# Three shifted terms in place of four for VectorE's exponentials, in a fused attention and MLP kernel

## The chip, the cores and the metric

The program runs on one core of a Trainium2 chip. The metric is the device time of one execution in microseconds (us), as a median over runs. The kernel before takes 758.89 us, the median of 3 runs (758.78 to 759.5).

## The reference

One transformer block in its parallel form: layer norm, then attention and an MLP side by side, summed with the input. The sizes are S = 2048 tokens, D = 512, H = 32 heads of 16 columns, F = 1792.

```python
xn = layernorm(x)
q, k, v = split(xn @ wqkv)                      # 32 heads of 16
p = softmax(q @ k.T * 16**-0.5)                 # 32 x 2048 x 2048 scores
attn = (p @ v) @ wo
y = layernorm(xn)
mlp = gelu(y @ w1 + b1) @ w2 + b2
return x + attn + mlp
```

So 134 million exponentials have to be taken, and that is what the kernel is built around.

## The kernel before

**Units and tiles.** Heads are taken four at a time. A *group* g is four heads against 512 queries (there are 32 groups), and a *tile* (g, k) is one group against 128 keys: four score blocks of 128x512, one for each head, which the text calls *units*. There are 32 x 16 x 4 = 2048 units. TensorE computes a unit's scores into one PSUM bank (`qk`, L1162), four row strips at a time. The softmax isn't normalised in advance: V has a column of ones beside its 16 (18 columns a head in `va`), so the sum of the exponentials comes out of the same product, and the result is divided by it later (`build_opost`, L1524).

**Two engines take the exponential.** ScalarE takes two or three units in one instruction (`build_tile`, L1382, output `p_sb`), in alternating pairs of banks, and each unit's weights are then multiplied with V (`build_pv`, L1180). VectorE takes whole tiles in another way (`build_dve`, L1467, and `dve_terms`, L1488). It adds a level to the scaled score and stores it as int16 (L1479, one *conversion* for each unit). Read as fp16, those bits are a stepwise linear 2**x. Three more copies, shifted by constants (L1500, one *shift* of 128x2048 for each term), have their kinks elsewhere, and the sum of the four is a smoother exponential. The sum is never formed: all four go into the product with V, one PV row (four matmuls) for each term, two rows to a piece of work.

```python
TERMS = 4                                                       # L34
SHIFT = (0, 190, 422, 740)                                      # L35
rows = [(va[:, k, :], bits(ib[sl]))]                            # L1492
    rows.append((va[:, k, :], bits(tb[x])))                     # L1507
    if len(rows) == 2 or t == TERMS - 1:                        # L1508
        o = add("PE", pen(len(rows)), lambda rows=rows: pv(g, k, rows), ...)
```

The scores of a VectorE tile *ride*: with each of ScalarE's score tiles, TensorE computes one unit for VectorE into another bank (`ride`, L1259). `KD` (L517) lists the key blocks that VectorE may take in a group. ScalarE takes the others first, and then what is left in `KD`.

**What sets the order.** The kernel is written as operations with an engine, a duration, dependencies and resources. A planner (`_Plan.run`, L134) lists them by a greedy rule when the program is built, and a table of numbers (`PICK`, L645) overrides its choice at some steps. The chip then runs each engine's list in order, and semaphores hold the dependencies. The planner also places matmuls on zeros where TensorE would otherwise be idle (`fill`, L1825; the 128x128 ones of the start stand on L1852, the later ones on L1857), and a zero strip beside some score tiles (`zeros`, L1310).

**Buffers.** The shifted copies lie in a ring of `NTB` = 4 tiles (`tb`, L564); a shift waits until the PV row that read its slot last is done. Other rings: q of a pair of groups in `NQB` = 4 slots (L568), W1 columns in `NW1` = 5, attention outputs in `NON` = 8 (L525). GpSimd adds x and b2 into `acc` by DMA (`sums`, L1717) and checks the softmax sums (L1570 to L1573).

**The end.** The last group is divided on VectorE in two halves (`build_opost_last`, L1580: transpose, reciprocal, multiply, transpose). `build_final` (L1773) adds the last products with Wo to `acc` for four blocks of 128 tokens: for three of them an fp32 identity matmul puts `acc` into the bank (L1784) and ScalarE copies it out (L1805), for one VectorE adds it (L1802). A flag is summed (L1622), every engine reads it and branches past a general version of the kernel.

## Time and profile before

| what | value |
|---|---|
| median of 3 runs | 758.89 us |
| the profiled execution's own time | 758.38 us |
| its span in the trace | 756.6 us |
| TensorE busy | 724.6 us (96%) |
| VectorE busy | 708.1 us (94%) |
| ScalarE busy | 735.4 us (97%) |
| GpSimd busy | 54.8 us (7%) |

Busy time is the time in which at least one instruction of the engine ran. The span goes from the first instruction to the last, barriers at the end included; 1.8 us of the execution's time lie around it. Three engines are close to full, so a share alone doesn't tell which of them sets the time: that is read from who waits for whom, stage by stage.

### The profile page before, as it was taken

The page shows a single profiled execution, that of the slowest core. Times are in us where ns is not written, and L with a number is a line of the kernel's source. Part 1 is how long each engine was busy: PE and PEld are TensorE (multiplying, and loading weights), DVE is VectorE, ACT ScalarE, POOL GpSimd, SP SyncE. Part 2 cuts the span into 40 slices and gives each one's busy share as a digit, 9 for nine tenths or more (in the row PEclk, how much of TensorE's full clock was granted, in tenths as well). Part 3 has the DMA queues.
Part 4 walks back from the last instruction along what each step waited for, and adds up shares of the span by engine and source line. Part 5 has one row for each costly group of instructions (what it writes and reads, how often), then busy time and mean ns, then how long its engine had stood idle before and what let it go on. Part 6 is the DMA issues. An engine that isn't in the chain of part 4 may idle for free.

```text
span 756.6 us, 23209 instructions
## 1 busy us (share of the span) xinstructions
PE 724.6 (96%) x9898; PEld 244.0 (32%) x9900; DVE 708.1 (94%) x1217; ACT 735.4 (97%) x663; POOL 54.8 (7%) x93
## 2 busy tenths in 40 slices
PE   8999999999999999999999999999999899999997
PEld 3443333343332323333333333332233222333332
DVE  8999999999999997999999989889999999879995
ACT  6999999999999999999999999999999999999995
POOL 4400000000121000000110000000002000100010
PEclk9999999999999999999999999999999999999999
DMA  7334321111255111121243121222114001332001
GB/s 223 86 72 130 73 68 28 35 48 50 51 122 109 52 31 40 52 49 30 68 103 75 37 70 29 54 62 71 33 46 109 14 22 35 86 79 52 17 7 45
DMA packets 79067, 46.54 MB, mean 62 GB/s; under 512 B 53428, under 2 KB 70772, under 8 KB 78960
## 3 DMA queue, kind: packets, MB, share of 16 engines
q1 hardware_dynamic: 73392, 36.11, 18.1%
q0 software_dynamic: 4608, 8.39, 4.9%
q8 instruction: 78, 1.28, 0.7%
q10 hardware_dynamic: 960, 0.52, 0.2%
q14 instruction: 29, 0.24, 0.1%
HBM read 30.01 MB, written 7.19 MB: 49 GB/s over the span
## 4 chain that ended last, share of the span: by engine, by line
ACT 38%; PE 34%; DVE 15%; issue 12%; DMA 1%; POOL 0%; DVEq 0%; ACTq 0%; POOLq 0%
ACT p_sb L1382 33%; PE ps L1162 11%; PE ps L1180 11%; PE ps L604 9%; DVE it L1500 5%; DVE x_sb L1479 5%; ACT ht L1681 2%; DVE it L1479 1%; ACT ht L1700 1%; DVE ht L1669 1%; PE ps L1857 0%; DVE osb L1535 0%; PE ps L609 0%; DVE va L1062 0%; DMA ldram<-osb 0%
## 5 line engine op out<-in xcount | busy, mean ns | idle before, releaser
L1382 ACT ACTIVATE p_sb<-ps 128x1536 bf16<-128x1536 f32 (+1 forms) x619 | 695.3, 1271 | 6.3 <-PE ps L1162 4.4
L1162 PE MATMUL ps<-qz,kt 32*128 32x512 bf16 x2048 | 310.2, 382 | 21.8 <-ACT p_sb L1382 12.7
L1479 DVE TENSOR_SCALAR x_sb<-ps 128x512 int16<-128x512 f32 x420 | 277.8, 682 | 13.6 <-PE ps L1162 12.1
L1500 DVE TENSOR_SCALAR it<-x_sb 128x2048 int16<-128x2048 int16 x315 | 211.2, 685 | 2.9 <-PE ps L1180 1.8
L1162 PEld LDWEIGHTS <-kt 32*128 32x128 bf16 x2048 | 85.3, 91 | 275.8 <-issue 265.8
L1180 PE MATMUL ps<-p_sb,va 128*32 128x512 bf16 x1520 | 150.4, 388 | 1.0 <-DVE va L1062 0.4
L1180 PE MATMUL ps<-it,va 128*32 128x512 f16 x1692 | 137.8, 381 | 1.1 <-DVE va L1062 0.6
L1180 PEld LDWEIGHTS <-va 128*32 128x32 bf16 x3632 | 76.0, 94 | 132.1 <-issue 106.7
L1317 PE MATMUL ps<-ones_bf,zeros_bf 32*128 32x512 bf16 x297 | 106.5, 382 | 0.0
L1479 DVE TENSOR_SCALAR it<-ps 128x512 int16<-128x512 f32 x108 | 72.3, 682 | 5.3 <-PE ps L1162 5.2
L604 PE MATMUL ps<-w_sb,ht 128*32 128x512 bf16 x896 | 59.7, 381 | 0.0
L604 PE MATMUL ps<-yT,w_r 128*32 128x512 bf16 x896 | 58.1, 381 | 0.0
L1500 DVE TENSOR_SCALAR it<-it 128x2048 int16<-128x2048 int16 x81 | 54.5, 682 | 1.2 <-PE ps L1180 0.7
L1180 PE MATMUL ps<-x_sb,va 128*32 128x512 f16 x420 | 41.4, 384 | 0.1
L1721 POOL DMA_DIRECT2D wkv<-in_A_x_dram x16 | 11.9, 741 | 297.7 <-DVE ot L1735 266.6
L1669 DVE TENSOR_SCALAR ht<-ps,b_sb 128x512 bf16<-128x512 f32 x40 | 29.8, 744 | 2.2 <-PE ps L604 2.1
L1317 PEld LDWEIGHTS <-zeros_bf 32*128 32x128 bf16 x297 | 25.9, 91 | 10.5 <-issue 9.3
L604 PEld LDWEIGHTS <-w_r 128*32 128x32 bf16 x896 | 21.0, 96 | 24.7 <-issue 10.0
L604 PEld LDWEIGHTS <-ht 128*32 128x32 bf16 x896 | 20.5, 96 | 23.2 <-issue 9.5
L1570 POOL TENSOR_SCALAR okt<-lc 128x128 f32<-128x128 f32 (+1 forms) x4 | 2.7, 666 | 314.3 <-DMA lc<-ldram 314.3
L1857 PE MATMUL ps<-ones_bf,zeros_bf 128*32 128x512 bf16 x252 | 22.8, 384 | 0.0
L1535 DVE COPY osb<-ps 128x512 f32<-128x512 f32 x31 | 21.2, 683 | 0.7 <-PE ps L1180 0.5
(98 smaller groups left out, 330.3 us busy)
## 6 DMA issues: line engine op xcount, KB each, us to landing
rlb<-rdram SPq DMA_DIRECT2D x31, 256.0 KB
w_r<-in_B_w_dram SPq DMA_DIRECT2D x56, 128.0 KB
wkv<-in_A_x_dram POOLq DMA_DIRECT2D x16, 256.0 KB, 3.5
wkv<-in_B_b_dram POOLq DMA_DIRECT2D x16, 256.0 KB, 4.1
qz<-zdram SPq DMA_DIRECT2D x30, 128.0 KB
ydram<-ys SPq DMA_DIRECT2D x16, 128.0 KB
zdram<-qc SPq DMA_DIRECT2D x15, 128.0 KB
w_sb<-in_B_w_dram SPq DMA_DIRECT2D x1, 1792.0 KB
```

Source lines behind the costliest of these rows:

```text
L604: I(nc.tensor.matmul(dst[32 * j:32 * j + 32], lhsT=lhsT[:, 32 * j:32 * j + 32], rhs=rhs, start=start, stop=stop, tile_position=(0, 32 * j)))
L1162: I(nc.tensor.matmul(ps[:, bank, :], lhsT=kt[lo:lo + 32, s // 2, k * P:(k + 1) * P], rhs=qz[lo:lo + 32, (qt * NB + s // 2) % NQB, s % 2, : ...
L1180: I(nc.tensor.matmul(ps[32 * j:32 * j + 32, o_bank[g], :], lhsT=vals[:, h * VS:h * VS + 32], rhs=wts(j), start=pv_done[g] == 1, stop=end, ...
L1317: I(nc.tensor.matmul(ps[:, o_bank[g], :], lhsT=zeros_bf[32 * j:32 * j + 32, :], rhs=ones_bf[32 * j:32 * j + 32, :], start=False, stop=Fals ...
L1382: exp_inst.append(I(nc.scalar.activation(p_sb[:, s0:s1, :].rearrange("p a b -> p (a b)"), ps[:, b0:b0 + n, :].rearrange("p a b -> p (a b)" ...
L1479: I(nc.vector.tensor_scalar(out=ib[sl][:, j, :], in0=ps[:, pool.bank(key), :], scalar1=LEVEL, scalar2=0.0, op0=ALU.add, op1=ALU.max))
L1500: I(nc.vector.tensor_scalar(out=tb[x].rearrange("p j q -> p (j q)"), in0=ib[sl].rearrange("p j q -> p (j q)"), scalar1=float(SHIFT[t]), sc ...
L1535: e0 = add("DVE", dve(QW), lambda: I(nc.vector.tensor_copy(osb[:, i2, :], ps[:, o_bank[g], :])), pvs + before, pr - 1000, rel=(o_done(g),))
L1669: I(nc.vector.tensor_scalar(out=hq[:, fc, :], in0=ps[:, misc.bank(key), :], scalar1=b1_sb[:, fc:fc + 1], scalar2=None, op0=ALU.add))
L1681: I(nc.scalar.activation(out=hv, in_=hv, func=AF.Gelu_apprx_tanh, scale=1.0))
L1721: xb_ = add("POOL", 1.0, lambda: I(nc.gpsimd.dma_start(out=acc[:, c, :], in_=x2[qi * P:(qi + 1) * P, :])), wait, pr - 30, lat=XL, nb=pr - 45)
L1857: I(nc.tensor.matmul(ps[32 * j:32 * j + 32, bank, :], lhsT=zeros_bf[:, 0:32], rhs=ones_bf[:], start=new, stop=new, tile_position=(0, 32 * ...
```

## The change

**Terms.** VectorE's exponential has three terms, with shifts 0, 342 and 683, and each shifted term is multiplied with its own weighted copy of V. The weights 1, 203/256 and 161/256 are applied to V when V leaves PSUM: for the key blocks in `KD`, VectorE writes two more copies into the new tile `vw`. GpSimd writes the weight into `vw`'s columns of ones, so that the sums are weighted too.

**Sizes.** `KD` goes from seven key blocks to five, so that `vw` has room; the rings shrink from 4 to 2 (`NTB`), 8 to 7 (`NON`), 5 to 4 (`NW1`) and 4 to 3 (`NQB`).

**End and start.** The last group is transposed at once and divided in two halves. Two blocks of tokens, not one, are added on VectorE, so that two identity matmuls are left. GpSimd executes a drain after its last DMA. The zeros of the start wait for an operation of another engine, and some are left out.

**Order.** The planner's constants and `PICK` are new.

```diff
-TERMS = 4
-SHIFT = (0, 190, 422, 740)
-LEVEL = 1024.0 * (15.0 - 2.41262)
+TERMS = 3
+SHIFT = (0, 342, 683)
+WEIGHT = (1.0, 203.0 / 256.0, 161.0 / 256.0)
+LEVEL = 1024.0 * (15.0 - 1.6403)
-    KD = (2, 4, 6, 8, 10, 12, 14)
+    KD = (6, 8, 10, 12, 14)
-    NPU, NI, NTB, NON, NW1 = 15, 5, 4, 8, 5
+    NPU, NI, NTB, NON, NW1 = 15, 5, 2, 7, 4
+    vw = const.tile([P, TERMS - 1, len(KD), VROW], BF, name="vw")
-    NQB = 4
+    NQB = 3
-    D1 = ((1, 7), (1, 8), (1, 13), (1, 14))
+    D1 = ((1, 6), (1, 8), (1, 12), (1, 14))
     PICK = {
-        29: 30, 69: 45, 83: 62, 93: 95, 101: 54, 104: 57, 107: 55, 117: 348, 118: 79, 128: 69, 130: 72,
+        30: 33, 43: 143, 65: 44, 93: 95, 99: 57, 108: 80, 131: 81, 136: 190, 138: 72, 139: 69, 141: 378,
...
+    def c_vw():
+        for t in range(1, TERMS):
+            I(nc.gpsimd.memset(vw[:, t - 1, :, 0:H * VS].rearrange("p k (h r) -> p k h r", r=VS)
+                               [:, :, :, DH:VS], WEIGHT[t]))
...
+    mk_vw = add("POOL", 1.6, c_vw, (r1_op[4],), 0.0)
...
+            def fvw(t, b=b, ks=ks, key=key, pool=pool):
+                x = KD.index(ks[0])
+                I(nc.vector.tensor_scalar(
+                    out=vw[:, t - 1, x:x + len(ks), 8 * b * VS:8 * (b + 1) * VS].rearrange(
+                        "p t (h r) -> p t h r", r=VS)[:, :, :, 0:DH],
+                    in0=ps[:, pool.bank(key), :].rearrange("p (t h r) -> p t h r", t=TQ, r=DH)
+                    [:, ks[0] % TQ:ks[-1] % TQ + 1:2],
+                    scalar1=WEIGHT[t], scalar2=None, op0=ALU.mult))
...
-        rows = [(va[:, k, :], bits(ib[sl]))]
+        rows = [(va_t(g, k, 0), bits(ib[sl]))]
-            rows.append((va[:, k, :], bits(tb[x])))
+            rows.append((va_t(g, k, t), bits(tb[x])))
+            deps.append(vw_of(g, k, t))
...
+        def f0():
+            I(nc.vector.transpose(out=ta[:], in_=ps[:, o_bank[g], :]))
+            I(nc.vector.reciprocal(out=rl_t[:], in_=tav[:, :, DH]))
...
+        def last():
+            I(nc.gpsimd.dma_start(out=acc[:, c, :], in_=b2_all, accum_op=ALU.add))
+            if qi == NT - 1:
+                I(nc.gpsimd.drain())
...
+        BARE = (1, 2)
-            dep = [acc_op[c], mk_idf] + h_use[(NQT - 1) % 2] + ([exp_prev[0]] if c else [])
-            if c != 2:
+            dep = [acc_op[c], mk_idf] + h_use[(NQT - 1) % 2] + ([qk_prev[0]] if c else [])
+            if c not in BARE:
-                if c == 2:
+                if c in BARE:
...
+            gate = max([x for x in I.trail if x[0] < t - 0.3 and x[1] in ("DVE", "ACT", "POOL")],
+                       key=lambda x: x[0], default=None) if t0 <= T0 and t > GATE else None
+            skip = COLD < t < WARM and len(got) % 2
```

Counted over the lists of instructions that the two programs have: conversions go from 528 to 556 (132 tiles to 139), shifts from 396 to 278, ScalarE's exponentials of 1536 columns from 282 to 276 and those of 1024 from 337 to 332 (1520 units to 1492). PV rows of VectorE's tiles go from 528 to 417, of ScalarE's from 380 to 373. Later zero matmuls (L1857 before) go from 252 to 332, zero strips from 297 to 323. Writes of `vw` on VectorE: 24, of which 8 have 128 columns and 16 have 256; on GpSimd there are 6 memsets.

VectorE after the first token block's output is added (`ot<-ps,wkv`, some 300 us into the program): conversions stand as `128x512`, shifts as `128x2048`, `osb` is the copy of a finished group. Before:

```order
L1735 TENSOR_TENSOR ot<-ps,wkv 128x512
L1479 TENSOR_SCALAR x_sb<-ps 128x512
L1535 COPY osb<-ps 128x512
L1479 TENSOR_SCALAR x_sb<-ps 128x512
L1500 TENSOR_SCALAR it<-x_sb 128x2048 x2
L1479 TENSOR_SCALAR x_sb<-ps 128x512
L1500 TENSOR_SCALAR it<-it 128x2048
L1479 TENSOR_SCALAR x_sb<-ps 128x512 x2
L1500 TENSOR_SCALAR it<-x_sb 128x2048
L1479 TENSOR_SCALAR x_sb<-ps 128x512 x2
L1500 TENSOR_SCALAR it<-x_sb 128x2048
```

And with the change:

```order
L1773 TENSOR_TENSOR ot<-ps,wkv 128x512
L1570 COPY osb<-ps 128x512
L1534 TENSOR_SCALAR it<-x_sb 128x2048 x2
L1513 TENSOR_SCALAR x_sb<-ps 128x512 x2
L1534 TENSOR_SCALAR it<-it 128x2048 x2
L1513 TENSOR_SCALAR x_sb<-ps 128x512 x2
L1534 TENSOR_SCALAR it<-x_sb 128x2048
L1513 TENSOR_SCALAR x_sb<-ps 128x512 x2
```

A tile now has two shifts to its four conversions, and the two slots of the ring are written in turn, so two to four conversions stand between two writes of a slot.

VectorE at the end of the program, from the last output copy before the final group. Before:

```order
L1735 TENSOR_TENSOR wkv<-ps,wkv 128x512
L1590 STREAM_TRANSPOSE ht<-ps 128x256
L1595 RECIPROCAL rl_t<-ht 128x8
L1596 TENSOR_TENSOR ht<-ht,rl_t 128x256
L1599 STREAM_TRANSPOSE ons<-ht 128x256
L1590 STREAM_TRANSPOSE ht<-ps 128x256
L1595 RECIPROCAL rl_t<-ht 128x8
L1596 TENSOR_TENSOR ht<-ht,rl_t 128x256
L1599 STREAM_TRANSPOSE ons<-ht 128x256
L1802 TENSOR_TENSOR yT<-ps,wkv 128x512
L1622 TENSOR_REDUCE flag_i<-ps 1x1
```

And with the change:

```order
L1584 TENSOR_TENSOR ont<-osb,rlb 128x512
L1534 TENSOR_SCALAR it<-it 128x2048 x2
L1622 STREAM_TRANSPOSE ht<-ps 128x512
L1623 RECIPROCAL rl_t<-ht 128x16
L1630 TENSOR_TENSOR ht<-ht,rl_t 128x256
L1633 STREAM_TRANSPOSE ons<-ht 128x256
L1630 TENSOR_TENSOR ht<-ht,rl_t 128x256
L1633 STREAM_TRANSPOSE ons<-ht 128x256
L1841 TENSOR_TENSOR yT<-ps,wkv 128x512 x2
L1656 TENSOR_REDUCE flag_i<-ps 1x1
```

The second half's transpose and reciprocal are gone from between the two multiplies, one more output block stands behind them, and the last tile's two shifts stand right ahead of the final transpose.

VectorE where the second quarter of V leaves PSUM (`va`), with the change; before, the row of `va` is followed by other work and `vw` isn't there:

```order
L849 TENSOR_SCALAR yT<-x_sb,mv,r_85 128x512 x3
L1074 CAST va<-ps 128x4x8x16
L1085 TENSOR_SCALAR vw<-ps 128x8x16 x2
L876 CAST xnT<-ps 128x4x128
```

The two copies for key block 6 are written before anything else of VectorE's, and the bank is given back only after them.

## Rows read from the trace of the kernel before

**Rows 1.** The page's first part: busy time, share of the span, instructions.

```profile
span 756.6 us, 23209 instructions
...
PE 724.6 (96%) x9898; PEld 244.0 (32%) x9900; DVE 708.1 (94%) x1217; ACT 735.4 (97%) x663; POOL 54.8 (7%) x93
```

**Rows 2.** Busy us by stretch: PE, PEld, DVE, ACT, POOL; clock, DMA share, GB/s.

```profile
13.00:60.00 47.00, 44.23 (x793) 18.11 (x792) 44.90 (x95) 45.40 (x50) 11.95 (x27) 1.00 0.31 83
60.00:105.00 45.00, 42.36 (x677) 15.01 (x681) 43.87 (x77) 43.69 (x41) 0.00 (x0) 1.00 0.35 92
...
150.00:200.00 50.00, 48.84 (x790) 17.25 (x787) 48.24 (x80) 49.84 (x45) 0.00 (x0) 1.00 0.19 50
...
sum 733.00, PE 708.69 PEld 236.15 DVE 694.22 ACT 726.68 POOL 48.23; mean PE 47.25 PEld 15.74 DVE 46.28 ACT 48.45 POOL 3.22
```

**Rows 3.** ScalarE's groups by shape: busy us, mean ns, idle before them.

```profile
L1382 ACT ACTIVATE p_sb<-ps 128x1536 bf16<-128x1536 f32 x282 | 424.2, 1504 | 2.3 <-PE ps L1162 1.9
L1382 ACT ACTIVATE p_sb<-ps 128x1024 bf16<-128x1024 f32 x337 | 356.9, 1077 | 4.1 <-PE ps L1162 2.5 <-ACT p_sb L1382 0.2
```

**Rows 4.** ScalarE's timeline, merged by line: start, length, instructions; both shapes in one.

```profile
99.56 161.54 ACT L1382 ACTIVATE p_sb<-ps 128x1536 bf16<-128x1536 f32 x142
```

**Rows 5.** VectorE's groups by shape.

```profile
L1479 DVE TENSOR_SCALAR x_sb<-ps 128x512 int16<-128x512 f32 x420 | 277.8, 682 | 13.6 <-PE ps L1162 12.1
L1500 DVE TENSOR_SCALAR it<-x_sb 128x2048 int16<-128x2048 int16 x315 | 211.2, 685 | 2.9 <-PE ps L1180 1.8
L1479 DVE TENSOR_SCALAR it<-ps 128x512 int16<-128x512 f32 x108 | 72.3, 682 | 5.3 <-PE ps L1162 5.2
L1500 DVE TENSOR_SCALAR it<-it 128x2048 int16<-128x2048 int16 x81 | 54.5, 682 | 1.2 <-PE ps L1180 0.7
...
L981 DVE TENSOR_SCALAR qz<-ps,mask 128x128 bf16<-128x128 f32 x1 | 0.3, 343 | 0.0
```

**Rows 6.** TensorE's timeline: a PV piece of one row, and one of two.

```profile
717.71 0.40 PE L1180 MATMUL ps<-p_sb,va 128*32 128x512 bf16 x4
...
718.90 0.60 PE L1180 MATMUL ps<-it,va 128*32 128x512 f16 x8
```

**Rows 7.** TensorE's groups by shape: the zero matmuls after the start.

```profile
L1857 PE MATMUL ps<-ones_bf,zeros_bf 128*32 128x512 bf16 x252 | 22.8, 384 | 0.0
```

**Rows 8.** Timeline of the end, all engines.

```profile
743.63 2.37 ACT L1382 ACTIVATE p_sb<-ps 128x1024 bf16<-128x1024 f32 x2
...
746.39 2.84 PE L1784 MATMUL ps<-wkv,ident_f 128*128 128x512 f32 x6
746.57 0.45 DVE L1590 STREAM_TRANSPOSE ht<-ps 128x256 f32<-128x256 f32 x1
...
749.28 0.45 DVE L1599 STREAM_TRANSPOSE ons<-ht 128x256 bf16<-128x256 bf16 x1
...
750.68 0.39 PE L604 MATMUL ps<-wo_l,ons 128*32 128x512 bf16 x4
...
751.19 0.69 DVE L1802 TENSOR_TENSOR yT<-ps,wkv 128x512 bf16<-128x512 f32 x1 [1.46 <-PE ps L604]
```

**Rows 9.** The closing line of the program: duration min/median/max, first and last start.

```profile
L1909 POOLq DRAIN  x3: 40/107/2683, 753.1 to 756.3; - x3
L1909 SPq DRAIN  x3: 7/7/13, 754.8 to 756.0; - x3
```

**Rows 10.** Stretches behind the last matmul; columns as in rows 2.

```profile
753.00:754.00 1.00, 0.00 (x0) 0.00 (x0) 0.00 (x0) 0.00 (x0) 0.00 (x0) 0.73 0.22 70
754.00:755.00 1.00, 0.00 (x0) 0.00 (x0) 0.00 (x0) 0.00 (x0) 0.00 (x0) 0.50 0.11 25
```

**Rows 11.** Timeline of the start: VectorE and GpSimd.

```profile
6.43 0.16 DVE L825 TENSOR_SCALAR wv<-mv 128x2 f32<-128x2 f32 x1
...
6.67 0.79 POOL L829 TENSOR_TENSOR r<-wv,mhalf 128x2 f32<-128x2 f32 x1 [0.60 <-DVE wv L825]
...
7.50 0.74 DVE L846 TENSOR_SCALAR yT<-x_sb,mv,r 128x512 bf16<-128x512 bf16 x2 [0.59 <-POOL r L829]
```

More of the change, by code (lines that the diff above doesn't have):

```diff
@@ L200, in run @@
             op.end, op.at = end, t
+            self.trail.append((end, op.eng, self.last.get(op.eng)))
             free[op.eng] = end
@@ L1065, in fve, with va_t, vw_of @@
                     in_=ps[:, pool.bank(key), :].rearrange("p (t h r) -> p t h r", t=TQ, r=DH)))
+            ks = [k for k in KD if k // TQ == tq]
+            free = (pool.giver(key),) + ((one,) if b else ())
             va_op[b, tq] = add("DVE", dve(QW), fve, (m, mk_va, mk_ok), pr - 500,
-                               rel=(pool.giver(key),) + ((one,) if b else ()))
+                               rel=() if ks else free)
+            def fvw(t, b=b, ks=ks, key=key, pool=pool):
[6 more added lines that the diff above has]
+                    scalar1=WEIGHT[t], scalar2=None, op0=ALU.mult))
+            o = va_op[b, tq]
+            for t in range(1, TERMS if ks else 1):
+                o = vw_op[b, tq, t] = add(
+                    "DVE", dve(len(ks) * P), lambda t=t, f=fvw: f(t), (o, mk_vw), pr - 500,
+                    rel=free if t == TERMS - 1 else ())
     def va_of(g, k):
         return va_op[g % NS // 2, k // TQ]
+    def va_t(g, k, t):
+        return va[:, k, :] if t == 0 else vw[:, t - 1, KD.index(k), :]
+    def vw_of(g, k, t):
+        return vw_op[g % NS // 2, k // TQ, t]
     blocks = [(g, kg) for kg in range(FO) for g in range(2)] + [
@@ L1723, in sums @@
             nb=pr - 45)
-        return add("POOL", 1.0, lambda: I(nc.gpsimd.dma_start(
-            out=acc[:, c, :], in_=b2_all, accum_op=ALU.add)), (xb_,), pr - 20, lat=XL)
+        def last():
+            I(nc.gpsimd.dma_start(out=acc[:, c, :], in_=b2_all, accum_op=ALU.add))
+            if qi == NT - 1:
+                I(nc.gpsimd.drain())
+        return add("POOL", 1.0, last, (xb_,), pr - 20, lat=XL)
     def heads(qt, bs, cs):
@@ L1848, in fill, with fn @@
                         continue
[L1850 removed]
+            gate = max([x for x in I.trail if x[0] < t - 0.3 and x[1] in ("DVE", "ACT", "POOL")],
+                       key=lambda x: x[0], default=None) if t0 <= T0 and t > GATE else None
+            skip = COLD < t < WARM and len(got) % 2
+            def fn(opened=o_open[-1] if o_open else None, spot=spot, gate=gate, skip=skip):
                 if t0 <= T0:
[L1852 to L1853 removed]
+                    if skip:
+                        return None
+                    m = I(nc.tensor.matmul(ps[:, OB, :], lhsT=zeros_bf[:], rhs=ones_bf[:],
+                                           start=True, stop=True))
+                    if gate:
+                        tc.add_manual_dep(m.ins, gate[2].ins.name, SYNC_DEP, reason="its turn")
+                    return m
                 bank = spot[0] if spot else o_bank[opened]
```

60 lines of the change are left out of this document (30 added, 30 removed), and 57 rows, old and new, of the table PICK.

## The prediction

> **What bounds the kernel now.** I read the page's busy times first, to see which engines are candidates [rows 1]: ScalarE with 97% of the span, TensorE with 96%, VectorE with 94%. That leaves it open, so the busy times by stretch come next [rows 2]. From 150 to 200 us ScalarE works 49.84 of 50 us, TensorE 48.84, VectorE 48.24. Over the 733 us from 13 to 746 it works 726.68; TensorE 708.69, some of it on zeros; VectorE 694.22. ScalarE's idle time of 6.3 us is the least, and it falls mostly early: 1.6 of 47 us up to 60 us, 1.3 of 45 us up to 105 us, where VectorE is at 96% and 97%. The groups of ScalarE say what ended it [rows 3]: 6.4 us ahead of all 619 exponentials, mostly a wait for the scores (L1162). So ScalarE's exponentials set the time, TensorE and VectorE sit just under it, and a change pays by what it takes off ScalarE, provided that the other two still feed it. What is left of the span is a start of some 11 us and an end of some 10 us behind the last exponential, two chains of their own.
>
> **ScalarE.** By the counts of the two programs it gives 28 units away: 6 exponentials of three units, 5 of two. The price of a unit comes from a long stretch without a gap [rows 4]: 142 exponentials, 71 of each shape, so 355 units, in 161.54 us, 0.455 us a unit. (The 1504 and 1077 ns of [rows 3] overlap their neighbours and are no price.) 28 x 0.455 = **12.7 us less** on the engine that sets the time.
>
> **VectorE.** It takes 7 tiles more and still works less. 118 shifts go, at 0.685 us each: 80.8 us less. 28 conversions come, at 0.682: 19.1 us more [rows 5]. The 24 writes of `vw` have no row; their ends are 0.343 us, the nearest scaled copy out of PSUM of 128 columns, and 0.682, the conversion of 512 [rows 5]. I take 0.343 for the 8 narrow ones and 0.45 for the 16 of 256 columns, nearer to the narrow end: 9.9 us (8.2 to 16.4). The sum is 51.8 us less, 708.1 to some 656. The `vw` writes of the first head pair, some 2.5 us, fall into the full stretch before 105 us; the first four VectorE tiles, which lie there too, have one shift less each, 2.7 us. I set the two against each other and count nothing.
>
> **TensorE.** PV rows of VectorE's tiles go from 528 to 417, of ScalarE's from 380 to 373: 118 rows less. A piece of two rows lasts 0.60 us and one of a single row 0.40 [rows 6], so a row is worth about 0.2 us: 24 us less. The zeros grow from 252 to 332 matmuls, 22.8 us by their group [rows 7], so 7 us more by the mean; the zero strips lie beside scores. TensorE ends some 17 us lower. Neither engine is the bound, so this counts for nothing by itself; what it can do is to feed ScalarE in better time. Of the 6.3 us of idle, 2.9 lie before 105 us, where VectorE was full. I take half of that back, **1.5 us**; the ends are a gain of all 6.3 and, since the new order was not seen on the chip, a loss of as much.
>
> **The end.** The last exponential ends at 746.0 [rows 8]. Three identity matmuls then hold TensorE for 2.84 us, up to 749.2; VectorE has the second half divided at 749.73; the last product starts at 750.68, the added block leaves VectorE at 751.88. With the change there are two identity matmuls (1.9 us, to 748.3 or, with four products ahead, 748.5), and on VectorE one transpose of 512 columns takes the place of two of 256 at 0.45 [rows 8]. At 0.7 to 0.9 us for that one, 0.25 for the reciprocal and 0.88 for a half, the halves stand at some 748.5 and 749.35. The products behind them end near 750.0 rather than 751.07, and VectorE's second addition near 750.8 rather than 751.88, although it has two to do: **1.05 us less** (0.4 to 1.5).
>
> **The drain.** The program closes with a drain on GpSimd that starts at 753.1 and lasts 2683 ns, to 755.8, while SyncE, which has the most to wait for, is at its own drain at 754.8 [rows 9]. So GpSimd holds the closing barrier back by 0.95 us. The other two drains of GpSimd last 107 and 40 ns, and no DMA of GpSimd stands behind the new drain. I take it that the long one is then done in the last block, where GpSimd is idle nearly throughout, and that the closing one is short: **0.95 us less** (0 to 0.95). Behind the new drain stand the checks of the sums and the flag; 2.7 us there are hidden, since GpSimd's work is 55 us in all [rows 1].
>
> On what a drain costs the Trainium skill speaks against this change: "VectorE: DVE Perf Modes", section "The DRAIN you can't avoid", calls the drains at a program's start and end a constant of about 12 ns on all five engines. By that page the early drain would bring nothing, and the sum would stand 0.95 us higher. The row disagrees for GpSimd, 2683 ns, and agrees for SyncE, 7 to 13 ns.
>
> **The start.** The second normalisation pair waited for a small addition at 6.43, which stood behind a wide operation, and for GpSimd's 0.79 us from 6.67; its tiles were written from 7.50 [rows 11]. The addition now stands first, so the pair can come some 0.45 us earlier, and the first scores need it. **0.4 us less**; the ends are 0.6 less and, with zeros that now wait and are partly left out, 1.0 more. The 6 memsets of `vw` on GpSimd stand ahead of the third group's rsqrt and cost at most 2 us there; they come where GpSimd works 12 of 47 us [rows 2], so nothing. A ring slot fewer for q and W1 leaves a pair of groups (733/16, some 45 us) for loads: nothing.
>
> **The sum.** 758.38 (the profiled execution, 0.5 under the median of the runs) - 12.7 - 1.5 - 1.05 - 0.95 - 0.4 = 741.8, say **742.0 us**. By the ends of the unknown terms the likeliest case reaches from 737.0 to 747.0 (not all ends fall together).
>
> **Rivals.**
> *The other engines' slack reaches ScalarE in full.* All 6.3 us of its idle go, which is 4.8 beyond the forecast: 737. If the price of a unit fell too, since small delays of the scores may hide in it, each 1% (0.455 to 0.450) would be 7 us on the 1492 units that are left; half a per cent gives 733.5. For it: 52 us less on VectorE, 17 on TensorE. Against it: from 150 to 200 us, with VectorE at 96%, ScalarE has no idle to give [rows 2], and pieces of TensorE's other work still stand between scores.
>
> *The smaller ring gives part back.* A shift must now wait for the PV row that read the slot two shifts before. Before, with four slots, 396 shifts waited 4.1 us in all [rows 5]. If the wait becomes 0.3 us for each of 278, it is 83 us, about VectorE's whole slack (742 - 656 = 86): conversions come late, their banks too, and TensorE's scores with them. Half of ScalarE's 12.7 us given back leaves 748, all of it 755.
>
> *Slower: the same stall, past its point.* The ring is the place, VectorE's list the mechanism: 86 us of slack over 139 tiles are 0.62 us a tile, and each 0.1 us beyond it costs 14 us. From 0.75 us a tile on the gain is gone; at 0.9 the time is 742 + 0.28 x 139 = 781. For it: the two last rows of a tile are read by TensorE, which runs in order, 1 to 2 us after the shift. Against it: two to four conversions, 1.4 to 2.7 us, stand between two writes of a slot.
>
> *Slower: TensorE's clock.* The granted clock is 1.00 in every stretch up to 753, and 0.50 from 754 on [rows 2, 10], the lower of the two levels (1.2 of 2.4 GHz), after the last matmul at 751. TensorE now has 17 us less to do. If the clock fell in the middle, its work, some 690 of 718 us, would take twice as long, so each us of the course at the lower level costs about 0.95: 17 us of it eat the gain, and 24 give 765. Against it: the 80 more zeros stand in the idle places. The Trainium skill, "TensorE: Matmul & The Clock Gate", section "What's actually happening", has the clock follow how busy the engine has been lately; by this rule the change makes a fall likelier, and the trace agrees that idleness brings one, with 0.50 in the stretch from 754 [rows 10].
>
> *The change doesn't do what it says.* If the drain stays long at the close, the time is 743; that lies within the forecast.
>
> **How the numbers follow.** A measurement of this kernel can tell about 0.2%, 1.5 us, from no change. Forecast 0.66; slack in full (733.5 to 737) 0.10; ring gives part back 0.13, of which 0.09 still faster and 0.04 within 0.2%; ring slower 0.06; clock 0.05, of which 0.04 slower. The range of 736.0 to 748.5 holds the forecast, some of the slack case and a little of the ring's, 0.8 together. Faster 0.86, same 0.04, slower 0.10.
>
> **What would show it.** Right: ScalarE busy about 722 us (one copy fewer at the end), and idle ahead of the exponentials near 5 us; VectorE near 656 us; shifts waiting for TensorE for less than 30 us in all; last exponential at about 731.5; closing drain of GpSimd under 0.2 us; end of the span some 8.6 us behind the end of the last exponential (10.6 before); clock 1.00 up to the last matmul. Wrong: VectorE's shifts or conversions with waits of tens of us, ScalarE idle by more than 12 us between 13 us and the last exponential, matmul stretches with a clock under 1.

## The result, and the profile after

The changed kernel takes **747.13 us** in the median (four executions: 745.2, 746.58, 747.69, 747.86) against 758.87 us before (758.78 to 759.5): a ratio of 0.984, 95% interval 0.9819 to 0.986, so 1.5% faster. The forecast was 742.0 with a range of 736.0 to 748.5. The sign is right and the time lies in the range, but 5.1 us of the expected 16.9 didn't come. The profiled execution is the shortest of the four, 745.2 us with a span of 743.4; I compare it with the one of before (758.38), and deal with the 1.9 us between it and the median by themselves. The spread is wider: 2.7 us over four executions, 0.7 before.

The page's first part of the changed kernel, as [rows 1]:

```profile
span 743.4 us, 22413 instructions
...
PE 711.3 (96%) x9530; PEld 239.3 (32%) x9530; DVE 668.1 (90%) x1150; ACT 722.2 (97%) x651; POOL 56.0 (8%) x97
```

ScalarE's groups by shape, the answer to [rows 3]: busy us, mean ns, then the idle time just before them and what ended it.

```profile
L1416 ACT ACTIVATE p_sb<-ps 128x1536 bf16<-128x1536 f32 x276 | 418.5, 1516 | 3.0 <-PE ps L1196 2.0 <-PE ps L1214 0.3
L1416 ACT ACTIVATE p_sb<-ps 128x1024 bf16<-128x1024 f32 x332 | 355.1, 1084 | 5.0 <-PE ps L1196 4.1
```

The busy times by stretch, as [rows 2] (columns: PE, PEld, DVE, ACT, POOL, granted clock, DMA share, GB/s):

```profile
13.00:60.00 47.00, 43.70 (x771) 17.23 (x770) 43.83 (x94) 44.36 (x49) 13.78 (x33) 1.00 0.28 81
...
150.00:200.00 50.00, 47.72 (x697) 16.32 (x693) 46.59 (x78) 49.98 (x45) 0.00 (x0) 1.00 0.18 47
```

ScalarE's work fell to 722.2 us, as the count of units says. Its idle time ahead of the exponentials rose instead of falling, from 6.4 to 8.0 us. In the first stretch alone it is 1.0 us more (45.40 us of work in 47 before, 44.36 now), and VectorE has only 1.07 us less to do there.

VectorE's groups, as [rows 5], with the new `vw` writes:

```profile
L1513 DVE TENSOR_SCALAR x_sb<-ps 128x512 int16<-128x512 f32 x440 | 289.9, 683 | 24.0 <-PE ps L1196 21.5 <-PE ps L1351 1.4
L1534 DVE TENSOR_SCALAR it<-x_sb 128x2048 int16<-128x2048 int16 x220 | 149.1, 684 | 4.0 <-PE ps L1214 2.5
L1513 DVE TENSOR_SCALAR it<-ps 128x512 int16<-128x512 f32 x116 | 78.0, 685 | 9.8 <-PE ps L1196 9.1 <-PE ps L1351 0.3
L1534 DVE TENSOR_SCALAR it<-it 128x2048 int16<-128x2048 int16 x58 | 39.4, 689 | 0.8 <-PE ps L1214 0.5
...
L1085 DVE TENSOR_SCALAR vw<-ps 128x256 bf16<-128x256 f32 x16 | 6.1, 415 | 0.0
...
L1085 DVE TENSOR_SCALAR vw<-ps 128x128 bf16<-128x128 f32 x8 | 1.9, 281 | 0.0
```

VectorE stood idle ahead of the shifts for 4.8 us in all, 3.0 of them put down to TensorE, against 4.1 before: the ring of two slots shows no cost in these waits.

The end, as [rows 8], and the closing drains, as [rows 9]:

```profile
727.80 6.91 ACT L1416 ACTIVATE p_sb<-ps 128x1536 bf16<-128x1536 f32 x6
...
735.27 0.72 DVE L1622 STREAM_TRANSPOSE ht<-ps 128x512 f32<-128x512 f32 x1 [1.10 <-PE ps L1214]
735.30 1.99 PE L1823 MATMUL ps<-wkv,ident_f 128*128 128x512 f32 x4
...
738.10 1.29 DVE L1841 TENSOR_TENSOR yT<-ps,wkv 128x512 bf16<-128x512 f32 x2
```

```profile
L1958 POOLq DRAIN  x3: 34/45/107, 740.6 to 743.1; - x3
L1958 SPq DRAIN  x3: 7/7/13, 742.5 to 742.8; - x3
```

The last exponential ends at 734.7 us (746.0 before). The end of the span stands 8.7 us behind it in place of 10.6. The sum of the two profiled executions closes: 758.38 - 12.9 (the exponentials' busy time, 695.3 to 682.4) + 1.6 (idle time ahead of them, 6.4 to 8.0) - 1.9 (the end) = 745.2.

So two questions are left: why relief on VectorE and TensorE fed ScalarE no better, and where the longer executions lose up to 3 us. My theory at this point: only ScalarE's units count, and its idle time is made of scores that stand behind other pieces in TensorE's order. Rivals: the relief is worth something, but a wait eats it; or TensorE's clock falls.

### The profile page after: what moved, and what is told of

Its sections match the earlier page's. It is cut to its first block, busy times and chain, and to the rows that moved or that the text cites. A ratio compares the mean times of both kernels' runs of the same rounds, so it can differ in the third digit from the quotient of the medians.

```text
span 743.4 us, 22413 instructions
## 1 busy us (share of the span) xinstructions
PE 711.3 (96%) x9530; PEld 239.3 (32%) x9530; DVE 668.1 (90%) x1150; ACT 722.2 (97%) x651; POOL 56.0 (8%) x97
## 4 chain that ended last, share of the span: by engine, by line
PE 41%; ACT 40%; issue 12%; DVE 6%; DMA 0%; POOL 0%; ACTq 0%; DVEq 0%
ACT p_sb L1416 36%; PE ps L1196 15%; PE ps L1214 13%; PE ps L608 11%; ACT ht L1715 2%; ACT ht L1734 1%; DVE x_sb L1513 1%; DVE it L1534 1%; DVE stats L816 1%; PE ps L1905 1%; PE ps L613 1%; DVE it L1513 1%; DMA ydram<-ys 0%; ACT L1416 0%; ACT L1715 0%
## 5 line engine op out<-in xcount | busy, mean ns | idle before, releaser
L1416 ACT ACTIVATE p_sb<-ps 128x1536 bf16<-128x1536 f32 (+1 forms) x608 | 682.4, 1280 | 8.0 <-PE ps L1196 6.1
L1196 PE MATMUL ps<-qz,kt 32*128 32x512 bf16 x2048 | 317.2, 382 | 22.8 <-ACT p_sb L1416 15.7
L1513 DVE TENSOR_SCALAR x_sb<-ps 128x512 int16<-128x512 f32 x440 | 289.9, 683 | 24.0 <-PE ps L1196 21.5
L1534 DVE TENSOR_SCALAR it<-x_sb 128x2048 int16<-128x2048 int16 x220 | 149.1, 684 | 4.0 <-PE ps L1214 2.5
L1351 PE MATMUL ps<-ones_bf,zeros_bf 32*128 32x512 bf16 x323 | 116.1, 383 | 0.0
L1214 PE MATMUL ps<-it,vw 128*32 128x512 f16 x1112 | 107.7, 381 | 0.8 <-DVE it L1534 0.4
L1214 PEld LDWEIGHTS <-va 128*32 128x32 bf16 x2048 | 47.9, 94 | 94.4 <-issue 86.2
L1214 PEld LDWEIGHTS <-vw 128*32 128x32 bf16 x1112 | 32.0, 95 | 27.8 <-issue 15.1
L1534 DVE TENSOR_SCALAR it<-it 128x2048 int16<-128x2048 int16 x58 | 39.4, 689 | 0.8 <-PE ps L1214 0.5
L1905 PE MATMUL ps<-ones_bf,zeros_bf 128*32 128x512 bf16 x332 | 30.0, 382 | 0.0
```

Source lines behind the costliest of these rows:

```text
L1196: I(nc.tensor.matmul(ps[:, bank, :], lhsT=kt[lo:lo + 32, s // 2, k * P:(k + 1) * P], rhs=qz[lo:lo + 32, (qt * NB + s // 2) % NQB, s % 2, : ...
L1214: I(nc.tensor.matmul(ps[32 * j:32 * j + 32, o_bank[g], :], lhsT=vals[:, h * VS:h * VS + 32], rhs=wts(j), start=pv_done[g] == 1, stop=end, ...
L1351: I(nc.tensor.matmul(ps[:, o_bank[g], :], lhsT=zeros_bf[32 * j:32 * j + 32, :], rhs=ones_bf[32 * j:32 * j + 32, :], start=False, stop=Fals ...
L1416: exp_inst.append(I(nc.scalar.activation(p_sb[:, s0:s1, :].rearrange("p a b -> p (a b)"), ps[:, b0:b0 + n, :].rearrange("p a b -> p (a b)" ...
L1513: I(nc.vector.tensor_scalar(out=ib[sl][:, j, :], in0=ps[:, pool.bank(key), :], scalar1=LEVEL, scalar2=0.0, op0=ALU.add, op1=ALU.max))
L1534: I(nc.vector.tensor_scalar(out=tb[x].rearrange("p j q -> p (j q)"), in0=ib[sl].rearrange("p j q -> p (j q)"), scalar1=float(SHIFT[t]), sc ...
```

## The experiments

Executions below are device times, each with its mean granted clock where that tells something. To find where two executions of one order part, I set the start of the n-th exponential of one trace against that of the other.

**The changed kernel again.** No edit.

> The changed kernel once more, to see its spread. Theory (ScalarE's work sets the time, and the rest of what differs between executions is idle time ahead of its exponentials): median 746 to 748, single executions up to 3 us apart, and a longer execution shows more than the 8.0 us of idle time ahead of the exponentials with the same 722 us of work. Rival (TensorE's clock): a longer execution shows stretches with a granted clock under 1.00 before the last matmul, and matmuls of more than their usual duration there. Rival (chance): all within 1 us of 747.

Median 747.55 us (745.03, 745.46, 747.55, 747.77, 748.53; mean clocks 0.999, 0.999, 0.997, 0.997, 0.995): the longer ones have the lower clock. The profiled one took 747.77 (span 746.0). Against the first trace the exponentials are within 0.6 us up to 402 us and 2.57 us later from 409 us on, to the end. Stretches of 2 us of this execution (columns as above):

```profile
400.00:402.00 2.00, 0.86 (x14) 0.16 (x7) 1.21 (x3) 2.00 (x3) 0.00 (x0) 1.00 0.50 110
402.00:404.00 2.00, 1.81 (x19) 0.34 (x18) 2.00 (x5) 1.50 (x2) 0.00 (x0) 1.00 0.07 16
404.00:406.00 2.00, 2.00 (x17) 0.38 (x16) 2.00 (x4) 1.38 (x3) 0.00 (x0) 0.51 0.07 16
406.00:408.00 2.00, 2.00 (x23) 0.57 (x15) 1.25 (x3) 1.38 (x1) 0.00 (x0) 0.63 0.05 12
```

And its timeline there (start, length, instruction; in brackets the idle time before it and what ended that):

```profile
395.10 0.55 SPq L1582 DMA_DIRECT2D rlb<-rdram  x1
...
400.79 0.69 DVE L1584 TENSOR_TENSOR ons<-osb,rlb 128x512 bf16<-128x512 f32 x1 [1.35 <-DMA rlb<-rdram]
401.40 0.69 DVE L1513 TENSOR_SCALAR x_sb<-ps 128x512 int16<-128x512 f32 x1
...
402.14 0.37 PE L1196 MATMUL ps<-qz,kt 32*128 32x512 bf16 x1 [1.27 <-DVE x_sb L1513]
...
402.84 1.45 ACT L1416 ACTIVATE p_sb<-ps 128x1536 bf16<-128x1536 f32 x1 [0.50 <-PE ps L1196]
```

Read from the top, this is a chain. `rlb` is the broadcast of a group's reciprocals, a DMA on SyncE's queue. VectorE reaches the multiply that needs it 1.35 us before it lands. Behind the multiply, in VectorE's order, stands a conversion that would give back a score bank; TensorE's next score needs that bank and waits 1.27 us; ScalarE waits 0.50 us for the score. Then the clock is granted at 0.51, the lower of the two levels (1.2 of 2.4 GHz), from 404 to 406 us, after a stretch in which TensorE was busy for 0.86 of 2.00 us, and the exponentials lose 2.5 us in all. In the first profiled execution VectorE didn't wait there, and the clock held. The page "TensorE: Matmul & The Clock Gate" of the Trainium skill, section "What's actually happening", has the clock follow how busy the engine has been lately; this trace agrees, but a longer stop at the same place, in the third profile of this kernel below, was followed by no fall.

**Before, with three terms in the same places.**

```diff
             def f2(t=t, x=x):
+                if t == 3:
+                    return
                 I(nc.vector.tensor_scalar(
...
+            if any(gone) and not end:     # the fourth term's PV row
+                continue
...
```

> The kernel before with its order, its 1520 ScalarE units and its 132 VectorE tiles, but the fourth term left out: no shift of 740 and no PV row for it (122 of 132 rows go, ten stay where they close a group's sum). So VectorE has some 83 to 90 us less and TensorE some 24 us less, ScalarE the same. Theory (only ScalarE's units count): 757 to 759.5, idle ahead of the exponentials no less than 4 us. Rival (the slack of the other engines reaches ScalarE): 6 to 12 us less, 747 to 753. Rival (clock): with TensorE under 700 us of 757 the granted clock falls somewhere, and the time is above 760.

The fourth term is left out of the result. Median 756.37 us beside 758.59 for the kernel before, ratio 0.9965 (0.9952 to 0.9978): 2.2 us off, with ScalarE's list untouched, and 3.0 by the shortest executions (755.11 and 758.15). That is more than the theory's bound and far from the 6 to 12 of the rival. The profiled one is the longest, 761.56 us, and shows what the relief costs when it goes wrong:

```profile
282.00:284.00 2.00, 0.87 (x14) 0.15 (x7) 2.00 (x5) 2.00 (x3) 0.00 (x0) 1.00 0.03 8
284.00:286.00 2.00, 1.53 (x21) 0.44 (x20) 0.57 (x2) 1.98 (x3) 0.00 (x0) 1.00 0.32 102
286.00:288.00 2.00, 1.33 (x13) 0.39 (x15) 1.87 (x3) 1.99 (x3) 0.00 (x0) 0.53 0.18 62
288.00:290.00 2.00, 2.00 (x20) 0.54 (x20) 1.29 (x2) 1.59 (x2) 0.00 (x0) 0.50 0.00 0
```

TensorE has idle places, the clock is at half from 286 to 300 us (the two last rows are its start), and the exponentials slip by 4.7 us against the trace of before (0.77 late at 288.6 us, 5.46 at 302.4). This stop was no DMA: TensorE waited 1.60 us at 284.47 for a bank from ScalarE's gelu.

**Without the third term's shift, and without its PV row.** Two kernels; the order is that of the changed one.

```diff
             def f2(t=t, x=x):
+                if t == 2:
+                    return
                 I(nc.vector.tensor_scalar(
...
```

> The changed kernel in its order without the third term's shift (139 instructions of VectorE); its PV row stays and reads the second term's slot. VectorE's work goes from 668 to some 580 us, TensorE's stays. Theory (the 8.0 us of idle time ahead of the exponentials are scores that stand behind other pieces in TensorE's order): no more than 1.5 us off the 747.1 of the changed kernel. Rival (scores of VectorE's tiles wait for its banks and hold the exponentials' scores up): 4 to 8 us off, 739 to 743.

```diff
+            if vals is None and not end and pv_done[g] > 1:    # the third term's PV row
+                continue
...
             for j in range(HS):
...
```

> The changed kernel in its order without the third term's PV row (130 of 139 rows of four matmuls, nine stay where they open or close a group's sum); the shift stays. TensorE's work goes from 711 to some 685 us, VectorE's stays. Theory (scores behind other pieces): idle ahead of the exponentials falls from 8.0 to 4 or 5 us, time 3 to 4 us less, 743 to 744. Rival (what is left of the idle time is the release of the banks by ScalarE itself): within 1 us of 747. Rival (clock): granted clock under 1.00 in some stretch, time above 749.

Both came out slower than the changed kernel: 749.01 us (747.91 to 750.22) without the shifts, where neither theory expected a loss, and 750.33 (747.09 to 752.9) without the rows, where only the clock's rival did. Both have waits for DMAs that the changed kernel has not, or has shorter. VectorE's and TensorE's waits for DMAs without the shifts, two rows of each table of waits (us in total, times, longest):

```profile
DVE rc L1579 <- DMA lc<-ldram: 1.6, 1, 1.6
...
DVE ys L900 <- DMA ydram<-ys: 0.9, 1, 0.9
```

```profile
PE ps L608 <- DMA w_r<-in_B_w_dram: 0.8, 1, 0.8
PE ps L608 <- DMA yT<-ydram: 0.6, 1, 0.6
```

The same table of TensorE has no DMA in the changed kernel, and VectorE's longest wait for one is 0.9 us. The waits of 0.6 us (`yT`, 229.6 us) and 1.6 (`lc`, 233.6) stand where the exponentials of this kernel fall back by 1.2 us, between 226 and 235. They fall back by some 2.9 in all; most of the rest comes in small steps with no wait for a DMA beside them, and its cause is open. Without the PV rows one wait is enough to stop everything (timeline, then the stretch):

```profile
230.79 1.90 PE L608 MATMUL ps<-yT,w_r 128*32 128x512 bf16 x16 [3.22 <-DMA yT<-ydram]
...
233.34 2.37 ACT L1419 ACTIVATE p_sb<-ps 128x1536 bf16<-128x1536 f32 x2 [4.12 <-PE ps L1196]
```

```profile
230.00:240.00 10.00, 9.21 (x87) 2.41 (x87) 5.88 (x11) 5.57 (x5) 2.29 (x3) 0.66 0.53 110
```

The exponentials were 1.06 us *ahead* of the changed kernel's at 228 us, 4.46 behind at 238, and 2.4 us more were lost at 405 to 412 us, behind the broadcast seen above. So one half of the theory holds, that relief is worth about 1 us where nothing stands in the way, and the other half falls: the rest is not TensorE's order alone. Without the PV rows it is a part of the lists that is tied to DMAs, and TensorE, which came to one early, stopped the others.

**That multiply four instructions later.** In VectorE's list it stands behind two conversions, a bias addition and a shift that stood behind it; nothing else moves.

```diff
+    late, until, kept = (2081, 2082, 2083, 2084, 2085), 2250, []
...
-            op.fn()
+            if op.seq in self.late:        # the multiply and its four copies
+                self.kept.append(op)
+            else:
+                op.fn()
+            if op.seq == self.until:       # a shift, four instructions on
+                while self.kept:
+                    o = self.kept.pop(0)
+                    self.cur = o.eng
+                    o.fn()
```

> The changed kernel with one VectorE instruction moved: the multiply by the broadcast reciprocals that VectorE reached at 400.79 us in the second run of the changed kernel, where it waited 1.35 us for its DMA, now stands behind the next four VectorE instructions (two conversions, a bias addition, a shift); the order of every other engine and of every queue stays. Theory (a late DMA holds VectorE, its conversions hold two score banks, TensorE stops for 1.27 us, the granted clock falls to 0.51, and 2.6 us are lost): no wait for this DMA, no stretch with a clock under 1.00 near 400 us, median 745.0 to 745.8, single executions within 1 us. Rival (the clock falls by itself, or something else spreads the executions): median 747 to 748 and a spread of 3 us as before.

Median 745.4 us (744.65, 745.0, 745.4, 745.88, 746.59), every mean clock 0.999 or 1.0, as the theory says, though the executions spread by 1.9 us and not by 1. The group of that multiply has no wait left (0.1 us in all), and the stretch that fell to 0.51 before:

```profile
400.00:410.00 10.00, 9.16 (x121) 3.18 (x114) 9.97 (x17) 9.93 (x10) 0.00 (x0) 1.00 0.22 50
```

**28 units given back to ScalarE.**

```diff
+            if i % 21 == 20 and i < 600:
+                I(nc.scalar.activation(p_sb[:, s0, :], ps[:, b0, :], AF.Exp, scale=1.0 / STEP))
```

> The changed kernel with 28 units of ScalarE's work given back: behind every 21st exponential its first unit of 512 columns is computed once more into the same place; nothing else changes. Theory (ScalarE sets the time at its start-to-start price, 0.427 us for 512 columns and 0.05 for an instruction, 0.477 in all): 13.4 us more, 758.5 where the clock holds, 758 to 761 in the median. Rival (part of it hides in ScalarE's 8 us of idle time, since TensorE gains on it): 5 to 10 us more, 752 to 757.

Median 763.87 us, shortest 761.32. Shortest against shortest (745.03) that is 16.3 us, 0.58 a unit: nearly the whole length of the instruction, 0.597, so nothing of it is hidden.

```profile
L1416 ACT ACTIVATE p_sb<-ps 128x1536 bf16<-128x1536 f32 (+1 forms) x608 | 684.6, 1259 | 12.4 <-PE ps L1196 11.0
L1420 ACT ACTIVATE p_sb<-ps 128x512 bf16<-128x512 f32 x28 | 16.7, 597 | 0.9
```

ScalarE's list sets the time; my price of 0.477, that of a unit within a longer instruction, was too low for an instruction of its own. (Whether the score banks, which are held longer, are a part of it wasn't tried.) The profiled execution (766.53) lost more at 410 to 420 us, behind a wait of 1.4 us for the same broadcast, with the clock at 0.66 there, and near 570 us.

**Without the early drain.**

```diff
-            if qi == NT - 1:
-                I(nc.gpsimd.drain())
```

> The changed kernel without the drain of GpSimd in the last block; the order stays. Theory (the 2.7 us that GpSimd needs behind its DMAs come back at the close and hold the barrier up): closing drain of GpSimd 2.6 to 2.8 us, the end of the span 9.6 us behind the end of the last exponential in place of 8.7, time 0.95 us more, 748.5 in the median (746.1 at the lowest). Rival (the closing drain is short because of something else in the change): closing drain under 0.2 us and no change.

```profile
L1956 POOLq DRAIN  x3: 40/107/2683, 741.0 to 744.2; - x3
L1956 SPq DRAIN  x3: 7/7/13, 742.9 to 744.0; - x3
```

The 2683 ns are back, the same as before the change, and the span ends 9.37 us behind the last exponential in place of 8.68: the drain is worth **0.69 us** here, since SyncE is later against GpSimd than it was. In the changed kernel the early drain itself starts at 679.0 us and lasts 5.8, not 2.7, and no other engine's wait is put down to it. By the Trainium skill, "VectorE: DVE Perf Modes", section "The DRAIN you can't avoid", a drain of a program's preamble or postamble is a constant of about 12 ns on every engine; these rows agree for SyncE and differ for GpSimd, 2683 ns without the early drain and 45 with it. The times alone say less: five executions of 746.27 to 746.41, all with a mean clock of 0.999 or 1.0. The profiled one did not stop near 400 us, although nothing there was edited, and its first exponential came 0.97 us late. Why none of the five runs longer is left open.

**The old end.** One identity block more, transposes in halves, one addition on VectorE; the drain stays.

```diff
...
-        BARE = (1, 2)
+        BARE = (2,)
...
```

> The changed kernel with the end as it was before: two transposes of 256 columns in place of one of 512, three identity matmuls ahead of the last products in place of two, one added block on VectorE in place of two. Theory (the chain behind the last exponential goes through the transposes, the halves and the last products): the end of the span 9.6 to 9.8 us behind the end of the last exponential in place of 8.7, time 1.0 us more, 748.5 in the median (746.1 at the lowest). Rival (the end is set by the closing barrier or the last output DMA alone): no change.

Median 747.96 us, shortest 746.46, 1.4 over the shortest of the changed kernel. VectorE's last addition ends 5.56 us behind the last exponential, 4.68 in the changed kernel: 0.88 us. The span's end is 2.1 us later, but 1.2 of that are SyncE's longer wait for its last writes in this execution (4.3 us from the last issue to its drain, 3.1 in the changed kernel), which the edit doesn't touch.

**Four on one chip.** The changed kernel, the later multiply again, the broadcast one place later, and a start without zeros.

> The changed kernel a third time, beside the next three on one chip. Theory (an execution loses 1.3 to 3.5 us when the broadcast of the reciprocals lands later than VectorE's multiply near 400 us): lowest 745.0 to 745.5, median 746.5 to 748, and in the profiled execution the wait at that multiply and the clock go together: no wait and 1.00, or 1 us or more of wait and a stretch under 0.9 within 10 us behind it. Rival (the clock falls by itself): a fall without the wait, or the wait without a fall.

> The kernel with that multiply behind the next four VectorE instructions, once more. Theory: median 745.0 to 745.8, lower than the median of the unmoved kernel beside it by 1 to 2.5 us, no wait for the broadcast near 400 us and no clock under 1.00 up to 733 us. Rival (the moved multiply has nothing to do with it): the same median and spread as the unmoved kernel.

```diff
-    late, until, kept = (2081, 2082, 2083, 2084, 2085), 2250, []
+    late, until, kept = (2080,), 2147, []      # the broadcast, behind the next load of W1
```

> The changed kernel with this one broadcast issued on SyncE's queue behind the next load of a piece of W1 (128 KB) instead of ahead of it; the order of all engines stays. Theory: the broadcast starts 0.4 to 1.5 us later, VectorE waits for it in every execution, by 1 us or more, the clock falls to one half behind it, lowest time above 746.3, median 747.5 to 749. Rival: lowest 745.0 to 745.5 as in the changed kernel, median unchanged.

```diff
-            skip = COLD < t < WARM and len(got) % 2
+            skip = COLD < t < WARM
```

> The changed kernel without the four zero matmuls that TensorE runs between 7 and 11 us (one ahead of the second transposes, two ahead of the first products of q and k, one ahead of the first scores). Theory (the two from 8.34 to 8.93 us hold the first products up, which is why the pair that comes 0.19 us earlier brings nothing): the first products start at 8.5 us in place of 8.77, the first exponential at 11.1 in place of 11.33, 0.2 us in all, which the times alone can't show. Rival (the products are paced by the clock of this stretch, and zeros keep it from being lower still): first exponential at 11.3 or later.

The changed kernel: 747.55 us (746.4 to 750.81). The later multiply beside it: **745.88 us** (744.73 to 746.9). The multiply's group in the profiled executions of the first, the third and the fourth kernel:

```profile
L1584 DVE TENSOR_TENSOR ons<-osb,rlb 128x512 bf16<-128x512 f32 x15 | 10.2, 681 | 1.8 <-DMA rlb<-rdram 1.8
```

```profile
L1593 DVE TENSOR_TENSOR ons<-osb,rlb 128x512 bf16<-128x512 f32 x15 | 10.2, 682 | 0.4 <-DMA rlb<-rdram 0.3
```

```profile
L1584 DVE TENSOR_TENSOR ons<-osb,rlb 128x512 bf16<-128x512 f32 x15 | 10.2, 680 | 1.7 <-DMA rlb<-rdram 1.7
```

Stretches of the first, around its wait:

```profile
402.00:404.00 2.00, 0.63 (x6) 0.11 (x5) 2.00 (x4) 1.05 (x2) 0.00 (x0) 1.00 0.17 37
404.00:406.00 2.00, 1.99 (x22) 0.52 (x21) 2.00 (x4) 1.93 (x2) 0.00 (x0) 1.00 0.12 29
```

The wait of 1.8 us in the first stopped TensorE for 1.74 us and cost 1.6, with the clock at 1.00; the one of 1.7 in the fourth stopped it for 1.61 us and cost 2.9, with 0.83 over 400 to 410 us. So the wait is there without the fall, against my expectation: the fall is an amplifier, not a part of the wait. Seven profiled executions have the multiply and the broadcast in their old places and all of VectorE's and TensorE's work around them: the changed kernel three times, the 28 units, the missing drain, the old end and the bare start. Four of them waited 1.3 to 1.8 us there, three 0.2 or less.

What goes with a late broadcast can be read from SyncE. Ahead of the broadcast SyncE waits for a write of 8 KB that takes the reciprocals to DRAM. Its waits for that write, in the first profile of the changed kernel and in the second (us in total, times, longest):

```profile
SPq L1582 <- DMA rdram<-rc: 3.3, 1, 3.3
```

```profile
SPq L1582 <- DMA rdram<-rc: 4.1, 1, 4.1
```

In the four executions in which VectorE waited, SyncE's wait is 4.1 to 4.4 us, and GpSimd had issued two loads of 256 KB (`wkv`) 0.80 and 0.07 us ahead of the write. In the three others it is 2.9 to 3.3 us, and the same two loads were issued 0.07 and 0.71 us behind the write. No run forces that order, so that it is the cause is not shown.

The broadcast behind a load missed its aim: it came only 0.3 us late, the profiled execution was the shortest of all (744.28 us), the others ran up to 747.93, median 746.45. So no late broadcast was forced, and the stop is shown by taking it away alone. Even that rests on the ten times and mean clocks of the later multiply: in both of its profiled executions the two loads were issued behind the write, so no profile shows the moved multiply meeting a late broadcast.

Over all, the changed kernel has a median of 747.55 us in 14 executions, six of them with a mean clock of 0.997 or less; the later multiply 745.64 in 10, none under 0.999. (The kernel before, in 31 executions beside the experiments, goes from 758.15 to 760.41 us, the changed one in 14 from 745.03 to 750.81, the later multiply in 10 from 744.65 to 746.9.) **It is the fastest version here**, with ratios of 0.9822 (0.981 to 0.9835) and 0.9824 (0.9809 to 0.984) to the kernel before.

The bare start (median 747.77 us, 744.6 to 750.17) brought the first products to 8.43 us and the first exponential to 10.78 (11.33 in the changed kernel), 0.3 us better than expected. The start of the later multiply's second profile, and then that of the bare start:

```profile
6.84 1.03 PE L622 MATMUL ps<-ident_bf,yT 128*128 128x128 bf16 x8
...
8.95 1.06 PE L1906 MATMUL ps<-ones_bf,zeros_bf 128*128 128x512 bf16 x2
...
12.62 1.02 ACT L1425 ACTIVATE p_sb<-ps 128x1024 bf16<-128x1024 f32 x1
```

```profile
6.87 0.72 PE L613 MATMUL ps<-ident_bf,yT 128*128 128x128 bf16 x8
...
8.43 0.39 PE L613 MATMUL ps<-xnT,wq_sb 128*128 128x128 bf16 x4
...
10.78 1.02 ACT L1416 ACTIVATE p_sb<-ps 128x1024 bf16<-128x1024 f32 x1
```

The same eight transposes take 1.03 us in one and 0.72 in the other, and two zeros then take another 1.06 ahead of the products. The first exponential comes at 12.62 instead of 11.33. Against the first profile of the same kernel, which started at 11.33 too, the first exponential is 1.29 us late and the last one 1.11. This, the start, is the second part of the spread.

It goes with the clock in all 14 profiled executions. Each trace keeps the stretches of the granted clock, and the first at the full level begins at 10.31 us here, and at 9.58 and 10.18 us in the two others whose first exponential is as late (without the early drain, and the changed kernel a third time). In all other profiled executions it begins between 4.7 and 7.5 us. The eight transposes took 1.00 to 1.06 us where they started ahead of it, in four executions, and 0.72 to 0.79 in the ten others. Before that first stretch the trace has no record, and the clock column reads 1.00. Why the clock rose so late in three executions is open: up to 4.5 us TensorE is busy for the same 2.87 us in all of them.

## Why the prediction was right, and where it missed

**ScalarE, 12.7 us: right.** Busy time 735.4 to 722.2 us, as forecast to 0.2 us. In reverse, 28 units cost at least what was taken off for them. What ScalarE gives away is worth its whole price.

**Idle time, -1.5 us: wrong.** "I take half of that back" took for granted that an engine with less to do feeds ScalarE sooner. Ahead of the exponentials it became 8.0 us, not near 5, so +1.6 in place of -1.5, and the last exponential ended at 734.7 us, not near 731.5. Of the range given there, a gain or a loss of all 6.3, the truth lies on the side of loss. What relief by itself is worth was measured on the kernel before, 2.2 us for 63 us of VectorE and some 120 PV rows; on the changed kernel both further reliefs made it slower. What in the new order holds the scores of the first 60 us by 1.0 us more was not tried apart.

**VectorE near 656 us: wrong, 668.1.** The terms were right: the groups' busy times fell by 51.4 us (conversions 350.1 to 367.9, shifts 265.7 to 188.5, `vw` 8.0 where 9.9 was taken), 51.8 forecast. But the page counts overlapping time once. Summed over all of VectorE's groups the busy time is 779.1 us before against 708.1 on the page, 729.1 after against 668.1: 71 us overlapped before, 61 after. A sum of group times mustn't be subtracted from the page's total. This changed no term of the time.

**TensorE, -17 us: came as -13.3** (724.6 to 711.3). The later zeros grew by 7.2 us (22.8 to 30.0), as taken; the groups of the PV rows fell by 16.5 (329.6 to 313.1), where 24 was taken. It was counted for nothing in the time.

**The end and the drain, 1.05 and 0.95 us: right in sum, 1.9.** VectorE's last addition ends 4.68 us behind the last exponential in place of 5.87: 1.19. The drain by itself is worth 0.69. The closing drain is 45 ns; the early one lasts 5.8 us where 2.7 was taken to be hidden, and is hidden all the same.

**The start, -0.4 us: wrong, 0.** The pair's tiles did come earlier, 7.31 us for 7.50, but TensorE ran two zeros first, and the products began at 8.77 us (8.53 before):

```profile
8.34 0.59 PE L1897 MATMUL ps<-ones_bf,zeros_bf 128*128 128x512 bf16 x2
...
8.77 0.39 PE L613 MATMUL ps<-xnT,wq_sb 128*128 128x128 bf16 x4
```

I had set zeros down in the range alone, and taken the gain as the likely case. Without the four zeros the first exponential came at 10.78 us, 0.55 earlier.

**The rivals.** The ring: no, 4.8 us of waits. Slack in full: no. The clock: it held in the first profiled execution, but in six of 14 executions it fell by what shows in the mean, and stretches under 1, which I had named as a sign of being wrong, stand in the second profile. I had it as a fall in the middle that costs 0.95 us for each us at the lower level. Measured, 14 us at half clock cost 4.7 us in the kernel before with three terms, a third of that; the zeros in TensorE's list may be part of the reason. And where a trace shows what came ahead of the fall, it isn't 17 us less work spread over the span but, in six of seven falls, one stop of TensorE of 1.1 to 3.2 us. (The seventh, at 568 us with the 28 units given back, follows 4 us in which it was busy for 2.88, with no stop above 0.9.) Stops of 1.02, 1.10 and 1.74 us were followed by no fall.

**What I hadn't in the list at all** is the wait behind most of the 1.9 us between the profiled execution and the median, as far as moving one multiply shows it: a DMA that VectorE can reach before it lands. That it gets there early because it has 50 us less work is argued only: the order is new as well, and the two weren't tried apart. The kernel before had one such wait, at another place (its timeline):

```profile
677.26 0.69 DVE L1549 TENSOR_TENSOR ons<-osb,rlb 128x512 bf16<-128x512 f32 x1 [1.68 <-DMA rlb<-rdram]
```

It was no shorter, but from 676 to 680 us TensorE still worked 4.00 of 4 us and ScalarE 3.92: whatever stood behind that multiply, the scores had what they needed. So here it isn't the length of such a wait that tells, but what stands behind the waiting instruction. I read VectorE's waits of before for the ring alone and asked this of none of them.

## What to carry to other kernels

A unit of work taken off the engine that sets the time pays in full; relief of the other two paid little here (2.2 us of 759) and can cost, where an engine that runs a fixed order reaches a DMA before it has landed. After such a change look for new waits on DMAs by engine, above all an engine that stands in front of a small DMA while others stand behind it, and move that one instruction back: here one multiply moved by four places gave 1.7 to 1.9 us of median. If executions spread where they didn't before, set the n-th instruction of the bounding engine in two traces against each other; the place where they part is where to look for the cause.

## What was not expected of the hardware

- GpSimd's closing drain took 2683 ns in the kernel before, in the one made from it and in the changed one without the early drain, to the nanosecond, and 45 ns wherever the engine had been drained in the last block.
- The stop by itself cost 1.6 us and with the fall of the clock 2.5 to 2.9. VectorE's wait was followed by a fall in three profiled executions (1.35, 1.36 and 1.69 us) and not in a fourth, where it was the longest (1.82). What decides that is open.
- The clock reached its full level at 4.7 to 7.5 us in eleven profiled executions and at 9.6 to 10.3 in three, on the same work of TensorE up to 4.5 us, and the clock column shows nothing of it. In eight profiled executions with the start of the changed kernel the first exponential came at 11.2 to 11.4 us, in the three late ones at 12.3 to 12.6.
- From the 240th exponential to the last, profiled executions of one order keep their distance to the first within about 0.1 us on either side of 400 us: the lists repeat almost exactly until a DMA comes late.
